# Expert weight buffers in two halves, one for each matmul, each refilled behind its own last use

## The chip, the cores and the metric

The kernel runs on one core of a Trainium2 chip. The metric is the device time of one execution in microseconds (us). A core has TensorE (PE in the profile; its weight loads are PEld), VectorE (DVE), ScalarE (ACT), GpSimd (POOL) and SyncE (SP), and 16 DMA engines that they share. SP and POOL issue the transfers here; each works through its own instructions in order, waits included.

## The reference

An attention with polynomial features feeds a mixture of experts, where each token goes to one expert.

```python
def _attn_ref(q, k, v, S1, S2):            # (4, 4, 1088, 32); S1, S2 (8, 32)
    phi = lambda x: outer(x @ S1.T, x @ S2.T)          # 64 features
    num = phi(q) @ (phi(k).T @ v)
    den = phi(q) @ phi(k).sum(seq) + 1e-6
    return num / den

def _moe_ref(x, w_gate, w_output_gate, w1, w2):   # x (4352, 128), E = 8, F = 1024
    logits = x @ w_gate
    e_idx = argmax(logits, axis=1)
    gate_w = softmax(logits)[e_idx]
    eom = sigmoid(x @ w_output_gate)
    for e in range(E):
        mask = e_idx == e
        h = maximum(x[mask] @ w1[e], 0)          # 128 -> 1024
        out[mask] = gate_w[mask] * eom[mask, e] * (h @ w2[e])   # 1024 -> 128
    return out
```

## The kernel before

The first part (to about 130 us) loads q, k and v in groups of columns, forms the attention output, computes the gates, and scatters each token's row, with its coefficient and its number, into a scratch array `xs` in HBM that is sorted by expert. A table is then made that says for each of `NT` = 41 tiles of 128 rows which expert it belongs to (`eti`) and where its rows begin (`bti`).

The second part walks over these 41 tiles with an order written out by hand. For each tile t:

- `rows(t)` (line 492, SP): reads the row address from `bti` (line 486) and loads 128 rows of 520 bytes into one of seven `xin` buffers. A buffer is free again when the scatter of the tile that used it has landed.
- `weights(t)` (line 496, SP): reads the expert from `eti` (line 486) and loads both weight matrices of the expert, 1 MB in 128 rows of 8 KB, into `wt[t % 3]`. The transfer has a condition: it is skipped when the buffer holds that expert already, that is when tile t-3 had the same one.
- `turn(t)` (line 502): TensorE transposes the rows, VectorE copies them to SBUF (line 504).
- `up(t)` (line 511): eight chunks of the first product into PSUM, read from `wt[t % 3][:, 0]`; then the relu on ScalarE (even tiles, line 513) or VectorE (odd tiles, line 515).
- `down(t)` (line 521): eight accumulating chunks of the second product, from `wt[t % 3][:, 1]`; ScalarE scales the result (line 523), and POOL scatters it to the output (line 524).

Each chunk of a product appears as two matmul instructions in the trace, so an up or a down has 16. The order for TensorE and SP is

```python
turn(0); turn(1); up(0)
for t in range(NT):
    turn(t + 2); up(t + 1); down(t)
    rows(t + NX)        # NX = 5
    weights(t + NW)     # NW = 3
```

Ahead of it stand `rows` 0 to 4 and `weights` 0 to 2 on SP, in turns. The three buffers are filled with the first expert's weights long before, at line 145, behind the loads of q, k and v.

Of the kernel before, what the change touches and what calls it, by code (L numbers as in the profile page):

```python
# [11 lines left out]
F32 = mybir.dt.float32  # L12
# [8 lines left out]
NW = 3  # L21
# [9 lines left out]
def kernel(  # L31
# [12 lines left out]
    nc = tc.nc  # L44
# [4 lines left out]
    E = w_d.shape[0]  # L49
    FC = (w_d.shape[2] // 2) // 128  # L50
# [9 lines left out]
    NT = (N + E * (TS - 1)) // TS  # L60
    PR = E * TS // 128

    consts = ctx.enter_context(tc.tile_pool(name="consts", bufs=1))
# [6 lines left out]
    def ps_t(name):  # L70
        return psum.tile([128, 512], F32, tag="t", bufs=2, name=name)

    def ps_w(name):
        return psum.tile([128, 2, 512], F32, tag="w2", bufs=2, name=name)

    def apart(group, ins):

        tc.declare_no_dep(ins.ins, group=group, reason="the rows are distinct")
        tc.add_to_no_dep_group(group, ins.ins)
# [8 lines left out]
    for i, x in enumerate((S1, S2)):  # L88
        own = slice(i * r, (i + 1) * r)
        if wide:  # L90
            x, dst, n = x.bitcast(I32), bits[own].rearrange("p (h d) w -> p h (d w)", h=2), 2 * D
# [48 lines left out]
            load_k(lead + g)  # L140


    wt = [consts.tile([128, 2, FC, 128], F32, tag=f"wt{i}", name=f"wt{i}") for i in range(NW)]
    for i in range(NW):
        nc.sync.dma_start(wt[i].rearrange("p a c x -> p (a c x)"), w_d[0])


    ident = consts.tile([128, 128], F32, tag="ident")
# [67 lines left out]
    ps = ps_t("ps_rows")  # L216
# [251 lines left out]
    eti = consts.tile([128, NT], I32, tag="eti")  # L468
# [14 lines left out]
    regs, xin, xTs, hTs = {}, {}, {}, {}  # L483

    def value(tab, t, top):
        return nc.values_load(tab[0:1, t:t + 1], engines=[mybir.EngineType.SP], min_val=0, max_val=top,
                              skip_runtime_bounds_check_because="the table is made within the bounds")

    def rows(t):
        at = value(bti, t, E * CAP - TS)  # L490
        xin[t] = work.tile([TS, W], F32, tag="xin", bufs=NX + 2, name="xin")
        nc.sync.dma_start(xin[t], xs[bass.ds(at, TS), :])

    def weights(t):
        regs[t] = value(eti, t, E - 1)
        nc.sync.dma_start(wt[t % NW].rearrange("p a c x -> p (a c x)"),
                          w_d[bass.ds(regs[t], 1)].rearrange("e p x -> p (e x)"),
                          cond=regs[t] != (regs[t - NW] if t >= NW else 0))

    def turn(t):  # L500
        ps = ps_t("ps_xs")[:, :TS]
        nc.tensor.transpose(ps, xin[t][:, :DM], ident)  # L502
        xTs[t] = work.tile([128, TS], F32, tag="xsT", bufs=3, name="xsT")
        nc.vector.tensor_copy(xTs[t], ps)  # L504

    def up(t):
        xT = xTs.pop(t)
        hTs[t] = work.tile([128, FC, TS], F32, tag="hT", name="hT")
        ps = ps_w("ps_h").rearrange("p a (c x) -> p (a c) x", x=TS)
        for c in range(FC):  # L510
            nc.tensor.matmul(ps[:, c], wt[t % NW][:, 0, c], xT, start=True, stop=True)  # L511
        if t % 2 == 0:
            nc.scalar.activation(hTs[t], ps, ACTF.Relu)  # L513
        else:
            nc.vector.tensor_scalar_max(hTs[t], ps, 0.0)  # L515

    def down(t):
        hT, x = hTs.pop(t), xin.pop(t)
        ps = psum.tile([TS, DM], F32, tag=("kvz", "rt")[t % 2], name="ps_y")
        for c in range(FC):  # L520
            nc.tensor.matmul(ps, hT[:, c], wt[t % NW][:, 1, c], start=(c == 0), stop=(c == FC - 1))  # L521
        y = work.tile([TS, DM], F32, tag="y", bufs=4, name="y")
        nc.scalar.activation(y, ps, ACTF.Copy, scale=x[:, DM:DM + 1])  # L523
        apart("out", nc.gpsimd.indirect_dma_start(  # L524
            out=out, out_offset=bass.IndirectOffsetOnAxis(ap=x.bitcast(I32)[:, DM + 1:DM + 2], axis=0),
            in_=y, in_offset=None, bounds_check=N - 1, oob_is_err=False))
# [3 lines left out]
    with tc.manual_schedule():  # L530
        for t in range(NX):
            rows(t)
            if t < NW:
                weights(t)
        turn(0)
        turn(1)
        up(0)
        for t in range(NT):
            if t + 2 < NT:
                turn(t + 2)  # L540
            if t + 1 < NT:
                up(t + 1)
            down(t)
            if t + NX < NT:
                rows(t + NX)
            if t + NW < NT:
                weights(t + NW)


# [34 lines left out]
```

## Time and profile before

| | |
|---|---|
| runs | 337.04, 331.01, 336.64 us; median 336.64 |
| profiled execution | 331.39 us, span 329.7 us, mean granted clock of TensorE 0.943 |
| TensorE busy | 270.0 us, 82% of the span |
| expert loop | about 139 to 322 us of the span |
| transfers | 44.49 MB in 18604 packets |

The span runs from the first to the last instruction of the core; the profiled execution's time has a little more around it. The granted clock is TensorE's, as a share of its full 2.4 GHz: 1.00 is 2.4 GHz and 0.50 is 1.2 GHz. In the chain of waits the pieces on TensorE lie end to end; in the timeline neighbouring matmuls overlap by a little, so that the same 16 matmuls show 1.79 us there and 1.95 us here. The name that a view gives for the releaser is inferred: at line 496 it names the transpose (line 502) that starts as the last matmul of a down ends.

### The profile page before, as it was taken

What the parts mean: (1) busy time and instruction counts of PE and PEld (TensorE: products, weight loads), DVE (VectorE), ACT (ScalarE), POOL (GpSimd) and SP (SyncE); (2) the same over time, 40 slices, a digit from 0 to 9 for tenths busy, and PEclk for the clock granted to TensorE, in tenths of its full rate; (3) what the DMA queues carried; (4) which work ended last, traced back from release to release, by engine and by line L of the source; (5) the groups of instructions that cost most, each with busy time, mean ns of one, the idle gap of its engine ahead of it and who ended that gap; (6) DMA issues with size and microseconds to landing.
All of it is one profiled execution on the core that took longest, in us unless ns stands there. A gap on an engine that the chain in (4) does not pass through costs nothing.

```text
span 329.7 us, 5562 instructions
## 1 busy us (share of the span) xinstructions
PE 270.0 (82%) x1990; PEld 245.2 (74%) x1990; DVE 103.3 (31%) x402; ACT 57.5 (17%) x108; POOL 77.9 (24%) x108
## 2 busy tenths in 40 slices
PE   1997899999999951199879888968978988889990
PEld 1996477778876651199869787858878988789990
DVE  4201235666566668022212112212111312222210
ACT  1000112212222110013112222202112222222220
POOL 3000001342334447112212221121122222212321
PEclk9999999999999965589979999989999999999995
DMA  5999998100010101212833748484473175671000
GB/s 149 252 252 245 245 245 354 35 32 10 25 35 24 35 33 48 90 40 81 262 126 101 243 134 278 151 288 140 136 227 110 45 230 204 187 253 34 16 2 0
DMA packets 18604, 44.49 MB, mean 135 GB/s; under 512 B 3258, under 2 KB 9148, under 8 KB 15504
## 3 DMA queue, kind: packets, MB, share of 16 engines
q1 hardware_dynamic: 16032, 39.09, 40.5%
q0 software_dynamic: 2544, 5.03, 4.4%
q8 instruction: 16, 0.26, 0.4%
q14 instruction: 12, 0.10, 0.1%
HBM read 60.06 MB, written 5.48 MB: 199 GB/s over the span
## 4 chain that ended last, share of the span: by engine, by line
PE 57%; DMA 25%; issue 7%; DVE 4%; POOL 3%; SPq 1%; ACT 1%; POOLq 0%; ACTq 0%
DMA wt<-in_w_dram 21%; PE ps_h L511 14%; PE ps_y L521 11%; PE ps_kvz L276 7%; PE ps_ab L249 6%; PE ps_nd L314 5%; PE ps_fa L294 5%; PE ps_fb L294 5%; PE ps_l L334 2%; POOL out_dram L524 2%; DMA xin<-xs 2%; DMA kT<-in_k_dram 1%; DMA xs<-pad,pai 1%; DVE kp L255 1%; PE ps_xt L329 1%
## 5 line engine op out<-in xcount | busy, mean ns | idle before, releaser
L511 PE MATMUL ps_h<-xsT,wt 128*128 128x128 f32 x656 | 85.2, 286 | 21.7 <-DMA wt<-in_w_dram 21.6
L511 PEld LDWEIGHTS ps_h<-xsT,wt 128*128 128x128 f32 x656 | 80.4, 200 | 25.4 <-issue 14.5
L521 PE MATMUL ps_y<-wt,hT 128*128 128x128 f32 x656 | 80.2, 276 | 0.0
L521 PEld LDWEIGHTS ps_y<-wt,hT 128*128 128x128 f32 x656 | 77.0, 193 | 0.0
L524 POOL DMA_INDIRECT out_dram<-y,xin x41 | 39.8, 971 | 149.9 <-ACT y L523 127.4
L396 POOL DMA_INDIRECT xs<-x,sloti x34 | 33.8, 995 | 93.9 <-DVE sloti L386 60.9
L504 DVE COPY xsT<-ps_xs 128x128 f32<-128x128 f32 x41 | 12.0, 292 | 105.2 <-PE ps_xs L502 105.2
L515 DVE TENSOR_SCALAR hT<-ps_h 128x1024 f32<-128x1024 f32 x20 | 24.5, 1225 | 41.8 <-PE ps_h L511 41.8
L513 ACT ACTIVATE hT<-ps_h 128x1024 f32<-128x1024 f32 x21 | 21.5, 1024 | 66.7 <-PE ps_h L511 66.7
L523 ACT ACTIVATE y<-ps_y,xin 128x128 f32<-128x128 f32 x41 | 15.1, 368 | 93.1 <-PE ps_y L521 93.1
L276 PEld LDWEIGHTS ps_kvz<-vt,kp 128*128 128x128 f32 (+1 forms) x144 | 22.8, 241 | 7.5 <-DVE kp L255 4.1
L276 PE MATMUL ps_kvz<-vt,kp 128*128 128x65 f32 (+1 forms) x144 | 23.7, 327 | 3.8 <-DVE kp L255 3.2
L502 PE MATMUL ps_xs<-ident,xin 128*128 128x128 f32 x41 | 11.6, 282 | 13.7 <-DMA xin<-xs 13.7
L249 PEld LDWEIGHTS ps_ab<-S12blk,kT 128*128 128x128 f32 x136 | 20.8, 241 | 2.5 <-DVE stepT L188 2.0
L249 PE MATMUL ps_ab<-S12blk,kT 128*128 128x32 f32 x136 | 20.9, 316 | 1.9 <-DMA kT<-in_k_dram 1.9
L294 PE MATMUL ps_fa<-qT,Sa 128*128 128x512 f32 (+1 forms) x36 | 19.1, 644 | 0.0
L314 PE MATMUL ps_nd<-kz,qp 128*128 128x66 f32 (+1 forms) x144 | 18.0, 273 | 0.1
L314 PEld LDWEIGHTS ps_nd<-kz,qp 128*128 128x128 f32 (+1 forms) x144 | 16.5, 186 | 1.6 <-issue 1.0
L294 PE MATMUL ps_fb<-qT,Sb 128*128 128x512 f32 (+1 forms) x36 | 17.3, 605 | 0.0
L255 DVE TENSOR_TENSOR kp<-ps_ab,b_sb 128x1024 f32<-128x1024 f32 (+1 forms) x9 | 10.5, 1166 | 21.7 <-ACT b_sb L252 21.7
L502 PEld LDWEIGHTS ps_xs<-ident,xin 128*128 128x128 f32 x41 | 6.0, 145 | 14.1 <-DMA xin<-xs 14.1
L306 DVE TENSOR_TENSOR qp<-a_sb,ps_fb 128x1024 f32<-128x1024 f32 (+1 forms) x9 | 10.5, 1161 | 12.8 <-PE ps_fb L294 12.8
(117 smaller groups left out, 146.8 us busy)
## 6 DMA issues: line engine op xcount, KB each, us to landing
wt<-in_w_dram SPq DMA_DIRECT2D x44, 1024.0 KB
kT<-in_k_dram SPq DMA_DIRECT2D x16, 256.0 KB, 8.8
qT<-in_q_dram SPq DMA_DIRECT2D x16, 256.0 KB, 7.5
xin<-xs SPq DMA_DIRECT2D x41, 65.0 KB, 4.0
vt<-in_v_dram SPq DMA_DIRECT2D x8, 260.0 KB, 6.2
out_dram<-y,xin POOLq DMA_INDIRECT x41, 4.5
xs<-x,sloti POOLq DMA_INDIRECT x34, 2.3
kT<-in_k_dram SPq DMA_DIRECT2D x2, 128.0 KB
```

The lines of the kernel that those rows point to most:

```text
L249: nc.tensor.matmul(ps[:, j * H + 2 * p:j * H + 2 * p + 2], kT[:, p, c * 128:(c + 1) * 128], S12blk, start=True, stop=True)
L276: nc.tensor.matmul(acc[b][:, p], s["kp"][p0:p0 + np_, j * H + 2 * p:j * H + 2 * p + 2].rearrange("s h i j -> s (h i j)"), vt[p0:p0 + np_, ...
L294: nc.tensor.matmul(ps[:, p, :n], S_.rearrange("p h i j -> p (h i j)"), qT[:, p, cols(cs)], start=True, stop=True)
L314: nc.tensor.matmul(ps[p0:p0 + np_, p, j], s["qp"][:, p, j * 128 + p0:j * 128 + p0 + np_], kvz_done[b][:, p], start=True, stop=True)
L396: apart("rows", nc.gpsimd.indirect_dma_start(out=xs[:, :], out_offset=bass.IndirectOffsetOnAxis(ap=sloti[:, j:j + 1], axis=0), in_=s["x"][ ...
L502: nc.tensor.transpose(ps, xin[t][:, :DM], ident)
L511: nc.tensor.matmul(ps[:, c], wt[t % NW][:, 0, c], xT, start=True, stop=True)
L513: nc.scalar.activation(hTs[t], ps, ACTF.Relu)
L515: nc.vector.tensor_scalar_max(hTs[t], ps, 0.0)
L521: nc.tensor.matmul(ps, hT[:, c], wt[t % NW][:, 1, c], start=(c == 0), stop=(c == FC - 1))
L523: nc.scalar.activation(y, ps, ACTF.Copy, scale=x[:, DM:DM + 1])
L524: apart("out", nc.gpsimd.indirect_dma_start(out=out, out_offset=bass.IndirectOffsetOnAxis(ap=x.bitcast(I32)[:, DM + 1:DM + 2], axis=0), in ...
```

## The change

Each buffer becomes two tiles, `wt[i][0]` for the first product and `wt[i][1]` for the second, 4 KB a partition each. `weights(t, a)` loads one half: 512 KB in 128 rows of 4 KB out of rows of 8 KB. The first half of tile t+4 is issued behind `up(t+1)`, the second half of tile t+3 behind `down(t)` and `rows(t+5)`. The expert is read from the table once, with the first half; both halves have the condition. The three preloads become six.

```diff
-    wt = [consts.tile([128, 2, FC, 128], F32, tag=f"wt{i}", name=f"wt{i}") for i in range(NW)]
+    wt = [[consts.tile([128, FC, 128], F32, tag=f"wt{a}{i}", name=f"wt{a}{i}") for a in range(2)] for i in range(NW)]
+
+    def half(a):
+        return slice(a * FC * 128, (a + 1) * FC * 128)
     for i in range(NW):
-        nc.sync.dma_start(wt[i].rearrange("p a c x -> p (a c x)"), w_d[0])
+        for a in range(2):
+            nc.sync.dma_start(wt[i][a].rearrange("p c x -> p (c x)"), w_d[0, :, half(a)])
...
-    def weights(t):
-        regs[t] = value(eti, t, E - 1)
-        nc.sync.dma_start(wt[t % NW].rearrange("p a c x -> p (a c x)"),
-                          w_d[bass.ds(regs[t], 1)].rearrange("e p x -> p (e x)"),
+    def weights(t, a):
+        if a == 0:
+            regs[t] = value(eti, t, E - 1)
+        nc.sync.dma_start(wt[t % NW][a].rearrange("p c x -> p (c x)"),
+                          w_d[bass.ds(regs[t], 1), :, half(a)].rearrange("e p x -> p (e x)"),
                           cond=regs[t] != (regs[t - NW] if t >= NW else 0))
...
-            nc.tensor.matmul(ps[:, c], wt[t % NW][:, 0, c], xT, start=True, stop=True)
+            nc.tensor.matmul(ps[:, c], wt[t % NW][0][:, c], xT, start=True, stop=True)
...
-            nc.tensor.matmul(ps, hT[:, c], wt[t % NW][:, 1, c], start=(c == 0), stop=(c == FC - 1))
+            nc.tensor.matmul(ps, hT[:, c], wt[t % NW][1][:, c], start=(c == 0), stop=(c == FC - 1))
...
             rows(t)
             if t < NW:
-                weights(t)
+                weights(t, 0)
+                weights(t, 1)
         turn(0)
         turn(1)
         up(0)
+        weights(NW, 0)
         for t in range(NT):
             if t + 2 < NT:
                 turn(t + 2)
             if t + 1 < NT:
                 up(t + 1)
+                if t + 1 + NW < NT:
+                    weights(t + 1 + NW, 0)
             down(t)
             if t + NX < NT:
                 rows(t + NX)
             if t + NW < NT:
-                weights(t + NW)
+                weights(t + NW, 1)
```

## Rows read from the trace of the kernel before

**Rows 1.** The page, parts 1 and 2: busy time and tenths in 40 slices.
```profile
PE 270.0 (82%) x1990; PEld 245.2 (74%) x1990; DVE 103.3 (31%) x402; ACT 57.5 (17%) x108; POOL 77.9 (24%) x108
PE   1997899999999951199879888968978988889990
```
**Rows 2.** The page, part 4: the chain of waits by line.
```profile
DMA wt<-in_w_dram 21%; PE ps_h L511 14%; PE ps_y L521 11%; PE ps_kvz L276 7%; PE ps_ab L249 6%; PE ps_nd L314 5%; PE ps_fa L294 5%; PE ps_fb L294 5%; PE ps_l L334 2%; POOL out_dram L524 2%; DMA xin<-xs 2%; DMA kT<-in_k_dram 1%; DMA xs<-pad,pai 1%; DVE kp L255 1%; PE ps_xt L329 1%
```
**Rows 3.** Waits on TensorE, 139 to 322 us: us in total, times, longest.
```profile
PE ps_h L511 <- DMA wt<-in_w_dram: 21.6, 16, 3.1
```
**Rows 4.** The SP queue's own waits, whole span.
```profile
SPq L496 <- PE ps_xs L502: 87.7, 38, 4.4
SPq L486 <- DVE bti L480: 83.6, 1, 83.6
SPq L492 <- DMA out_dram<-y,xin: 17.5, 17, 2.4
```
**Rows 5.** The chain in order of time, from 139 us: start, us, what.
```profile
139.83 2.94 PE ps_h L511 x16
...
150.14 0.11 PE ps_xs L502
150.25 1.79 PE ps_h L511 x16
152.03 1.79 PE ps_y L521 x16
...
153.85 4.82 DMA wt<-in_w_dram
158.67 0.14 issue
158.80 2.02 PE ps_h L511 x16
```
**Rows 6.** The two longest waits: chain, timeline, and a stretch (clock 0.50, DMA, GB/s).
```profile
168.87 3.24 PE ps_h L511 x16
172.11 2.20 PE ps_y L521 x16
...
213.86 6.71 DMA wt<-in_w_dram
...
220.71 3.62 PE L511 MATMUL ps_h<-xsT,wt 128*128 128x128 f32 x16 [3.09 <-DMA wt<-in_w_dram]
...
221.00:222.00 1.00, 1.00 (x6) 1.00 (x6) 0.00 (x0) 0.00 (x0) 0.00 (x0) 0.50 0.88 346
```
**Rows 7.** Weight issues in the SP timeline: skipped first, then first and last real.
```profile
136.80 0.11 SPq L496 DMA_DIRECT2D wt<-in_w_dram  x1
...
153.85 0.33 SPq L496 DMA_DIRECT2D wt<-in_w_dram  x1
...
291.86 0.33 SPq L496 DMA_DIRECT2D wt<-in_w_dram  x1
```
**Rows 8.** DMA: packets, then issues by line (count, KB each, us to landing).
```profile
DMA packets 18604, 44.49 MB, mean 135 GB/s; under 512 B 3258, under 2 KB 9148, under 8 KB 15504
...
kT<-in_k_dram SPq DMA_DIRECT2D x16, 256.0 KB, 8.8
xin<-xs SPq DMA_DIRECT2D x41, 65.0 KB, 4.0
```
**Rows 9.** Stretches: length; busy PE, PEld, DVE, ACT, POOL; clock, DMA share, GB/s.
```profile
10.00:20.00 10.00, 10.00 (x48) 10.00 (x49) 2.45 (x2) 0.53 (x2) 0.00 (x0) 1.00 1.07 250
142.60:153.80 11.20, 11.20 (x103) 11.20 (x102) 3.33 (x5) 2.79 (x4) 1.96 (x2) 1.00 0.16 37
196.00:210.70 14.70, 12.45 (x108) 11.82 (x107) 3.62 (x6) 2.50 (x5) 3.75 (x4) 1.00 0.74 240
252.00:264.00 12.00, 12.00 (x110) 12.00 (x110) 3.15 (x5) 3.12 (x5) 2.91 (x3) 1.00 0.13 35
...
200.50:201.00 0.50, 0.00 (x0) 0.00 (x0) 0.00 (x0) 0.00 (x0) 0.50 (x1) 1.00 1.37 266
201.00:201.50 0.50, 0.30 (x3) 0.33 (x4) 0.00 (x0) 0.00 (x0) 0.47 (x1) 1.00 0.94 147
201.50:202.00 0.50, 0.50 (x7) 0.50 (x6) 0.00 (x0) 0.00 (x0) 0.00 (x0) 1.00 0.57 164
```
**Rows 10.** Timeline: the last output copy.
```profile
320.99 0.37 ACT L523 ACTIVATE y<-ps_y,xin 128x128 f32<-128x128 f32 x1 [1.42 <-PE ps_y L521]
```
**Rows 11.** Single lines: duration in ns min/median/max, first and last start.
```profile
L521 PEldq EVENT_SEMAPHORE  x19: 51/51/51, 153.6 to 315.2; - x19
...
L496 SPq ALU_OP  x82: 37/39/54, 136.4 to 308.8; - x82
...
L486 SPq TENSOR_LOAD <-eti x41: 262/269/388, 136.1 to 308.4; - x41
```
**Rows 12.** The chain and the timeline just ahead of the first up.
```profile
136.06 0.28 SPq L486
...
139.35 0.47 PE ps_xs L502
```

## Prediction

> **What bounds the kernel now.** I read the page's first two parts first [rows 1]: TensorE (PE) is busy for 82% of the span, and its tenths fall below 9 mostly in the middle (the hand-over between the two halves of the kernel) and then again and again in the second half. The chain of waits [rows 2] names the cause: 21% of it is the transfer of expert weights (`wt<-in_w_dram`). That transfer exists only in the expert loop, so everything is decided in the stretch from about 139 us to 322 us. There [rows 3] the first product of the experts (line 511) waited 16 times for weights, 21.6 us together, the longest 3.1 us. The SP queue's own view [rows 4] shows the other end: SP stood 87.7 us at the weight issue (line 496) until TensorE was done with the buffer, and 17.5 us at the row loads (line 492) until an earlier scatter of results had landed.
>
> The chain in order of time tells how one stall is made [rows 5]. Without loads a tile costs 1.79 us for the first product ("up"), 1.79 for the second ("down"), and 0.11 for the transpose of the next rows ("turn"), 3.69 in all. At 153.85, when a down ends, a load is issued; it lands 4.82 us later and 0.14 us after that the up starts. Between the end of down(t), where the buffer comes free, and the start of up(t+3), which needs it, stand only turn, up, down, turn: 2 x 1.79 + 2 x 0.11 = 3.80 us. A load of about 5 us doesn't fit there, so nearly each pays about 1.1 to 1.4 us, and one that took 6.71 us paid 3.09 [rows 5, 6]. A stall costs more than the wait: the up after it shows 2.02 us in the chain instead of 1.79, and after the two longest waits 3.24 and 3.62 us [rows 6], at a granted clock of 0.50 (1.2 GHz instead of 2.4), after TensorE had stood idle.
>
> How many loads there are: of 41 weight issues those with unchanged expert are skipped. The real ones take about 0.33 us on SP, the skipped ones 0.08 to 0.11; the first and last real ones are at 153.85 and 291.86, and there are 21, three for each of seven experts (the first expert's are all skipped) [rows 7]. The packets agree: 18604 - 15504 = 3100 packets have 8 KB or more, and 24 loads (3 preloads and 21) x 128 rows of 8 KB are 3072, with 28 instruction packets the rest [rows 8]. From the order of real and skipped issues the experts have 5, 5, 4, 4, 4, 7, 4 and 8 tiles (the last with padding).
>
> **The change, part by part.**
>
> *Removed: the weight stalls.* A half of the first product is free at the end of up(t) and needed at up(t+3): three downs, two ups and three turns lie between, 5 x 1.79 + 3 x 0.11 = 9.28 us. The half of the second product is free at the end of down(t) and needed at down(t+3): three ups, two downs, three turns, again 9.28 us. Against 3.80 before, the time in hand is 5.5 us larger for both, and what must arrive first is half as large.
>
> What a half takes: in 196.0 to 210.7 three loads ran; the 16 DMA engines were busy 0.74 x 14.7 = 10.9 us [rows 9]. Row loads and scatters alone cost 0.13 x 12 = 1.56 us in 252 to 264, with 3.26 tiles, so 0.48 us a tile [rows 9]; four tiles take 1.9. The three loads are left with 9.0 us, 3.0 each, 1.5 for a half. The latency around it is 4.82 - 3.0 = 1.8 us [rows 5]. Alone a half lands 3.3 us after its issue, behind one other half 4.8, with a slow case like that of 6.71 us (1.9 more) 6.7: all under 9.28. So I take the remaining weight stall as zero. The bound on the other side: a half is moved in rows of 4 KB instead of 8, and the nearest row with smaller ones is the input stage, 2 KB rows (256 KB in 128 rows) at 250 GB/s with the engines full [rows 8, 9]. At that rate a half takes 0.524 MB / 250 = 2.1 us. Four-tile experts then need 6 x 2.1 + 1.9 = 14.5 us of engine time in 4 x 3.69 = 14.7 us: just full, and queues grow. I price that at up to 1.5 us for each of the four experts with four tiles: 0 to 6 us. I take 0, as 4 KB lies between the two rows, and even 2.1 us behind another 2.1 and 1.8 of latency are 6.0 of the 9.28 us.
>
> *The sum, end to end.* The first up starts its chain piece at 139.83 and takes 2.94 us (cold) [rows 5]. After it TensorE owes 40 ups, 41 downs and 39 turns: 81 x 1.79 + 39 x 0.11 = 149.3 us, so it is done at 142.77 + 149.3 = 292.1. Before, the last output copy, which starts as TensorE ends, began at 320.99 [rows 10]. Gain: 28.9 us. The stalls added up give nearly the same: 21.6 waits [rows 3], 14 x 0.23 = 3.2 for the slow ups, 1.45 + 0.41 + 1.83 = 3.7 for the work at the low clock [rows 5, 6], together 28.5. That no other engine is late next is shown by the stretches without loads: in 142.6 to 153.8 and 252 to 264 TensorE is busy throughout at 3.69 us a tile with the same relu, copies and scatters around it [rows 9]. What TensorE is fed from stays below that: SP's work per tile is two loads of a table value (0.27 each), the row issue (0.33) and now two weight issues with two ALU steps, a fused one and a move each (0.33 + 0.17), about 2.0 of 3.69 us [rows 11].
>
> *Added: a second skipped issue ahead of the loop.* Rows(1) stand behind weights(0) on SP, and up(0) behind turn(1). From the end of the table load (136.34) to the end of the skipped issue (136.91) 0.57 us pass [rows 7, 12]; the second half repeats that without the load. Bounds 0 and 0.6; I take +0.5, on the path, as TensorE waited for those rows until 139.35 [rows 12].
>
> *Added: a wait on TensorE for the second half* ahead of each down. A separate wait instruction is 51 ns; 19 of the 41 downs carry one already [rows 11], and the steady stretches show the same 1.79 with and without. Bounds 0 and 41 x 0.051 = 2.1 us; I take 0, since those rows are the nearest.
>
> *Moved: row loads.* Rows(t+5) now stand behind the first half's issue, so half a tile later (about 1.8 us), and the second half's issue stands behind them and behind their wait for the scatter of tile t-2, at most 2.4 us [rows 4]. Rows are needed three tiles on, 9.3 us, against 4.0 us to land [rows 8]; a second half 2.4 us late still has 6.9 us for 4.8. Being later, that wait is also shorter. Cost 0; without that cover it would be at most those 2.4 us a tile. The three preloads become six, on SP ahead of an 83.6 us wait for the tile table [rows 4]; cost 0.
>
> Span: 329.7 - 28.9 + 0.5 = 301.3. The profiled execution took 331.39, 1.7 us around its span, which gives **303.0 us**. It lies at the low end of the runs shown (331.01 to 337.04, median 336.64); the profile doesn't show where the other 5 us arise, so the range keeps them.
>
> **A rule that speaks against it.** The trace shows that loads don't pay their latency one after the other: from 200.5 to 202.0, while one 1 MB load lands at 201.1 and the next follows, the DMA share is 1.37, 0.94 and 0.57 and never near 0, and input loads of 256 KB land 8.8 us after issue while the queue moves 250 GB/s, which is several in flight [rows 8, 9]. The Trainium skill, page "DMA: Bandwidth & Descriptors", section "Rules for kernel authors", asks for at least 1 MiB per DMA, and its section "Anatomy of one DMA — SWDGE (gpsimd) path" gives each a fixed 2.0 us besides its bytes. By that figure, if nothing overlapped, an estimate for a half is 3.2 us, and the sum would be close to rival 1's. The overlap in the trace says that this isn't paid here.
>
> **The rivals.**
> 1. *Halves go one at a time, each with its own latency.* A half then holds the queue for 1.8 + 1.5 = T = 3.3 us, six for an expert 19.8 us against 14.7 for four tiles. From the first release (end of up(2): 142.77 + 3 x 1.79 + 2 x 0.11 + 0.5 = 148.9) 42 halves follow, with a pause at the seven-tile expert (25.8 - 6T), then one down and five tiles (20.2): TensorE ends at 194.9 + 36T = 313.7 instead of 321.0, the time is 324, at the edge of 2%; I count it as no change. Against it: the overlap above.
> 2. *The same, with the 2 KB rows' rate: slower.* T = 1.8 + 2.1 = 3.9, end at 335.3, so 14 us later than now: 346 us. The mechanism decides from T = 3.5 us on, where 194.9 + 36T equals 321.0. For it: small rows do move slower here (250 GB/s against 1.05 MB in 3.0 us, 350). Against it: the same overlap.
> 3. *Pipelined, but the engines are full with 4 KB rows*: 303 + 6 = 309 us, to 313. For it: the share of 0.74 already at four-tile experts.
> 4. *The change doesn't do what it says*: the first half is issued only when the down ends, SP being held. Then its room is 3.80 us again; a half alone takes 3.3, the second isn't needed before 5.6. Only the two slow loads would stall, with their cold clock: 303 + 3 = 306 us. For it: SP's in-order waits. Against it: every wait ahead on SP ends earlier on TensorE.
>
> **How the numbers follow.** Forecast 303 (300 to 308): 0.79. Rival 4: 0.06. Rival 3: 0.08. Rival 1: 0.04. Rival 2: 0.03. The range runs from 299 (the floor of TensorE's work less a little at the start) to 313, taking in rivals 3 and 4, the 2.1 us of waits and the spread of the runs; 0.93 by the cases. Faster by over 2%: 0.93; within 2% (about what a measurement of this kernel can tell from no change), rival 1: 0.04; slower: 0.03.
>
> **What would show it.** Right: TensorE's waits for weights fall from 21.6 us to under 3, all ups and downs after the first take 1.79 us in the chain, the clock stays at 1.00 from 143 us on, packets of 8 KB are gone and 48 x 128 of 4 KB appear, issues of first halves start at the end of ups, the DMA share in four-tile experts stays near 0.75. Wrong: waits at line 521 for weights, a share near 1 there (rival 3), landings that follow one another by over 3 us (rivals 1, 2), first halves issued at the end of downs (rival 4), or row loads that TensorE waits for.

## The result and the profile after

The change is faster: 307.92 us median (306.46 to 311.55, 4 runs) against 333.82 (329.04 to 337.04, 4 runs) in the same session; before has 334.95 over the eleven runs that were made with the last experiments (329.80 to 337.53). The ratio is 0.933 (95% interval 0.925 to 0.940), made from the undisturbed runs of each kernel alone (329.04 and 331.01 us against 306.46 to 308.40, on average 22.6 us apart), while the profiles of "before, again" and of the two kernels with the halves together, below, come from slower runs. The forecast was 303.0 against a profiled 331.39, which is 28.4 us and a ratio of 0.914. So direction and kind are right and the time lies in the range, 5 us above the forecast, at the upper end of the likeliest part of it (300 to 308).

The page of the changed kernel, parts 1 and 2 (busy time, tenths, granted clock; beside [rows 1]), and its DMA line ([rows 8]):

```profile
PE 265.9 (87%) x1990; PEld 243.1 (80%) x1990; DVE 103.3 (34%) x402; ACT 57.5 (19%) x108; POOL 77.5 (25%) x108
...
PE   0997979999999988402999999999999999999980
...
PEclk9999979899999999655899999999999999999997
DMA packets 22062, 44.50 MB, mean 146 GB/s; under 512 B 3642, under 2 KB 9532, under 8 KB 22032
```

From the twentieth slice on TensorE shows nothing but nines, up to the tail: the expert loop has no holes left. All packets are now under 8 KB. 22062 - 18604 = 3458 packets are new: 24 x 128 = 3072 from cutting each load in two, 3642 - 3258 = 384 of under 512 B (24 x 16, that is 16 for each of the 24 more transfers), and two of instructions. But the clock line has two dips in the first part, in the sixth and the eighth slice, that before's page hadn't.

The groups of instructions on TensorE by line (busy us, mean ns | idle before), and the SP queue's own waits from 144 to 290 us, beside [rows 3] and [rows 4]:

```profile
L516 PE MATMUL ps_h<-xsT,wt 128*128 128x128 f32 x656 | 81.8, 279 | 0.0
L526 PE MATMUL ps_y<-wt,hT 128*128 128x128 f32 x656 | 79.8, 275 | 0.0
```

```profile
SPq L501 <- PE ps_h L516: 15.8, 17, 1.1
SPq L501 <- PE ps_xs L507: 14.9, 36, 3.3
SPq L589 <- DMA out_dram<-y,xin: 11.5, 1, 11.5
SPq L496 <- ACT hT L518: 3.8, 14, 0.4
```

TensorE's wait for weights is 0.0 where it was 21.6 us. SP now waits for the end of ups (`ps_h`) as well as of downs, which is the first half being issued behind its own last use. And the 17.5 us that SP stood at the row loads for a scatter are gone: what is left there is 3.8 us on the relu's engine. That row becomes important below.

Two stretches of the expert loop (columns as in [rows 9]), the first over one four-tile expert:

```profile
182.70:197.40 14.70, 14.70 (x134) 14.70 (x133) 3.62 (x6) 3.52 (x6) 3.85 (x5) 1.00 0.81 244
148.00:298.00 150.00, 149.00 (x1334) 148.81 (x1333) 35.86 (x59) 36.34 (x62) 39.14 (x41) 1.00 0.59 180
```

In 14.7 us TensorE is busy for 14.7 us, at clock 1.00: the loop is bound by TensorE alone. The DMA share at a four-tile expert is 0.81; with 1.9 us for rows and scatters a half costs (0.81 x 14.7 - 1.9) / 6 = 1.67 us of engine time.

Where the 5 us went shows in the timeline at the seam (beside [rows 10] and [rows 12]):

```profile
139.63 0.36 SPq L496 DMA_DIRECT2D xin<-xs  x1
...
144.14 3.62 PE L516 MATMUL ps_h<-xsT,wt 128*128 128x128 f32 x16
...
297.04 0.37 ACT L528 ACTIVATE y<-ps_y,xin 128x128 f32<-128x128 f32 x1 [1.42 <-PE ps_y L526]
```

I cut each execution there, at the issue of the first sorted rows. Before, the first part took 135.66 us and the loop, up to the last output copy, 320.99 - 135.66 = 185.3. After, it is 139.63 and 297.04 - 139.63 = 157.4. The loop gained 27.9 us (forecast 28.9 - 0.5 = 28.4); the first part, in which no engine but SP has other instructions, lost 4.0; together that is 23.9. So two questions are left: what makes the gain in the loop, and whether the change or chance made the first part longer.

### The profile page after: what moved, and what is told of

It reads as the page before. It is cut to its first block, busy times and chain, and to the rows that moved or that the text cites. A ratio compares the mean times of both kernels' runs of the same rounds, so it can differ in the third digit from the quotient of the medians.

```text
span 305.7 us, 5829 instructions
## 1 busy us (share of the span) xinstructions
PE 265.9 (87%) x1990; PEld 243.1 (80%) x1990; DVE 103.3 (34%) x402; ACT 57.5 (19%) x108; POOL 77.5 (25%) x108
## 2 busy tenths in 40 slices
DMA packets 22062, 44.50 MB, mean 146 GB/s; under 512 B 3642, under 2 KB 9532, under 8 KB 22032
## 4 chain that ended last, share of the span: by engine, by line
issue 39%; PE 35%; POOL 13%; DVE 4%; DMA 3%; POOLq 1%; ACT 1%; SPq 1%; ACTq 0%
POOL out_dram L529 12%; PE ps_kvz L280 7%; PE ps_ab L253 6%; PE ps_fa L298 6%; PE ps_nd L318 6%; PE ps_fb L298 4%; PE ps_l L338 3%; DMA kT<-in_k_dram 1%; DMA xs<-pad,pai 1%; PE ps_xt L333 1%; POOLq L529 1%; PE ps_pos L372 1%; DVE kp L259 1%; DMA xin<-xs 1%; PE ps_pos L373 1%
## 5 line engine op out<-in xcount | busy, mean ns | idle before, releaser
L516 PE MATMUL ps_h<-xsT,wt 128*128 128x128 f32 x656 | 81.8, 279 | 0.0
L516 PEld LDWEIGHTS ps_h<-xsT,wt 128*128 128x128 f32 x656 | 78.4, 196 | 0.0
L280 PEld LDWEIGHTS ps_kvz<-vt,kp 128*128 128x128 f32 (+1 forms) x144 | 23.5, 245 | 8.1 <-DVE kp L259 4.4
L253 PEld LDWEIGHTS ps_ab<-S12blk,kT 128*128 128x128 f32 x136 | 20.8, 241 | 2.6 <-DVE stepT L192 2.1
L298 PE MATMUL ps_fa<-qT,Sa 128*128 128x512 f32 (+1 forms) x36 | 21.9, 728 | 0.0
L507 PEld LDWEIGHTS ps_xs<-ident,xin 128*128 128x128 f32 x41 | 6.0, 148 | 14.7 <-DMA xin<-xs 14.7
```

The costliest lines, as they stand in the source:

```text
L253: nc.tensor.matmul(ps[:, j * H + 2 * p:j * H + 2 * p + 2], kT[:, p, c * 128:(c + 1) * 128], S12blk, start=True, stop=True)
L280: nc.tensor.matmul(acc[b][:, p], s["kp"][p0:p0 + np_, j * H + 2 * p:j * H + 2 * p + 2].rearrange("s h i j -> s (h i j)"), vt[p0:p0 + np_, ...
L298: nc.tensor.matmul(ps[:, p, :n], S_.rearrange("p h i j -> p (h i j)"), qT[:, p, cols(cs)], start=True, stop=True)
L516: nc.tensor.matmul(ps[:, c], wt[t % NW][0][:, c], xT, start=True, stop=True)
```

## Experiments

Each kernel's loop is cut in the same way. "Waits" is TensorE's wait for weights in the loop.

| kernel | first rows issued | last output copy | loop | waits | time, median |
|---|---|---|---|---|---|
| before | 135.66 | 320.99 | 185.3 | 21.6 | 334.95 |
| before, again | 144.89 | 326.09 | 181.2 | 18.3 | 336.56 (one) |
| after | 139.63 | 297.04 | 157.4 | 0 | 307.92 |
| after, again | 143.50 | 300.40 | 156.9 | 0 | 310.80 (one) |
| split, halves together | 141.59 | 307.59 | 166.0 | 5.5 | 314.23 |
| the same, ten row buffers | 144.64 | 305.75 | 161.1 | 1.9 | 314.94 |
| split, second half first | 142.98 | 337.91 | 194.9 | 27.6 | 349.30 |
| four whole buffers | 141.30 | 298.61 | 157.3 | 0 | 309.05 |
| change, 2 KB rows | 139.41 | 295.92 | 156.5 | 0 | 307.52 |
| change, early start | 139.26 | 295.02 | 155.8 | 0 | 306.91 |

**Both kernels once more, for the first part.** No edit. Expected of before:

> The kernel before once more, for its first part alone. In the profiles so far the load of the first sorted rows is issued at 135.66 us before the change and at 139.63 us after it, though no instruction of TensorE stands in another order there. Theory 'by chance': the first part differs from execution to execution, because the granted clock falls at other places; this repeat lies anywhere from 134 to 142 us. Theory 'by the change' (six preloads of 512 KB in place of three of 1 MB): it lies at 135.7 within 1 us, and its first part has no stretch at clock 0.50 between 10 and 115 us. The expert loop, from that issue to the last output copy, is 185 us within 3 by both.

And of after:

> The kernel after the change once more, for its first part alone. Theory 'by chance': the issue of the first sorted rows lies anywhere from 134 to 142 us. Theory 'by the change': at 139.6 within 1 us, with stretches at a low clock around 42 and 53 us again. The expert loop from there to the last output copy is 157.4 us within 1 by both.

Measured: the first rows are issued at 144.89 us in before and at 143.50 in after. Both lie above the 134 to 142 us that "by chance" had expected, and before's loop of 181.2 us lies outside 185 within 3; after's 156.9 is as expected. The theory "by the change" fails all the same: the kernel with three whole preloads took 9.2 us longer than its first profile, more than the one with six halves, and the one with four whole preloads (below) came to 141.30. Two stretches of before's first profile, and then the same two of its repeat (columns as in [rows 9]; the last three are clock, DMA share, GB/s):

```profile
42.00:44.00 2.00, 2.00 (x11) 1.28 (x10) 0.00 (x0) 0.00 (x0) 0.00 (x0) 1.00 1.12 252
10.00:116.00 106.00, 101.08 (x597) 81.00 (x597) 51.14 (x226) 18.54 (x40) 23.49 (x24) 1.00 0.52 135
```

```profile
42.00:44.00 2.00, 2.00 (x4) 0.97 (x4) 0.00 (x0) 0.00 (x0) 0.00 (x0) 0.50 1.09 223
10.00:116.00 106.00, 100.15 (x548) 78.78 (x549) 46.06 (x202) 16.43 (x35) 19.60 (x20) 0.94 0.52 133
```

Same kernel, same work: at 42 us the clock is 1.00 in one and 0.50 in the other (1.2 instead of 2.4 GHz), and over 10 to 116 us the mean is 1.00 against 0.94. At half clock for 12% of 106 us that is 12.7 us at half speed, some 6.4 us of work, if TensorE sets the pace there. That would account for most of the 9.2 us; TensorE's last matmul of that part starts at 124.6 us in one and 132.3 in the other.

Over all ten profiled executions the first rows are issued from 135.66 to 144.89 us: with whole preloads at 135.66, 141.30 and 144.89, with halves at 139.26 to 144.64. By and large, the later they are, the lower is the mean clock over 10 to 116 us: 1.00 at 135.66, 0.97 at 139.26 to 139.63, 0.95 at 141.30 and 141.59, and 0.92 to 0.94 from 142.98 on. The first fall also comes ahead of what the change alters. Here are the stretch and the first preload, of the change and then of the kernel with four whole buffers:

```profile
42.40:45.70 3.30, 3.30 (x5) 1.24 (x5) 0.00 (x0) 0.00 (x0) 0.00 (x0) 0.50 1.11 241
...
46.08 5.14 SPq L149 DMA_DIRECT2D wt<-in_w_dram  x6
```

```profile
40.40:46.60 6.20, 6.20 (x19) 4.13 (x18) 0.00 (x0) 0.79 (x1) 0.00 (x0) 0.50 1.10 231
...
46.68 3.35 SPq L145 DMA_DIRECT2D wt<-in_w_dram  x4
```

Nine of the ten profiles are at 0.50 from 42.9 to 43.7 us, and no preload is issued before 45.4, so preloads, whole or halved, don't make this fall. The tenth, with no such stretch up to 110 us and the shortest first part of all, is the profile on which the forecast rests. That the clock accounts for the longer first part is read from these ten executions; no run changed the clock alone.

**Halves together, where the whole load stood.** Does the gain need the first half's own place, or does splitting the buffer do it?

```diff
                 up(t + 1)
-                if t + 1 + NW < NT:
-                    weights(t + 1 + NW, 0)
             down(t)
             ...
             if t + NW < NT:
+                weights(t + NW, 0)
                 weights(t + NW, 1)
```

(`weights(NW, 0)` ahead of the loop goes too.)

> Split buffers, but both halves are issued one behind the other where the whole load stood, behind down(t) and rows(t+5). Theory 'room': the first half needs no place of its own, as its buffer is free since up(t) and SP comes to it about 1.2 us after down(t-1); its room is 9.3 - 1.8 - 1.2 = 6.3 us against 3.3 to 4.9 to land, so TensorE waits for weights under 1 us in all and the expert loop takes 157 to 159 us, the whole some 307 us. Rival 'place': without its own place behind the up the first half comes with the second at the end of the down, room 3.8 us; the slower loads stall, 5 to 15 us in all, the loop takes 163 to 175 us.

Measured: the loop takes 166.0 us and TensorE waits 5.5 us for weights; ratio 0.940 (0.926 to 0.955). The theory "room" as I priced it fails, and "place" fits the numbers. The reason stands in the SP queue's waits of this kernel from 140 to 300 us:

```profile
SPq L501 <- PE ps_xs L507: 38.9, 32, 3.0
SPq L496 <- DMA out_dram<-y,xin: 20.8, 16, 2.4
```

and in its timeline at one of the six stalls, first SP, then TensorE:

```profile
182.54 2.06 SPq L501 DMA_DIRECT2D wt<-in_w_dram  x2
185.68 0.33 SPq L496 DMA_DIRECT2D xin<-xs  x1
186.69 1.59 SPq L501 DMA_DIRECT2D wt<-in_w_dram  x2
...
192.43 2.02 PE L516 MATMUL ps_h<-xsT,wt 128*128 128x128 f32 x16 [0.72 <-DMA wt<-in_w_dram]
```

The pair at 182.54 is done at 184.60. The row load behind it goes only at 185.68, when the scatter that holds its buffer has landed, and the next first half at 186.69. It lands 5.6 us later (0.14 us ahead of the up's start at 192.43), and TensorE has stood 0.72 us. So SP was held by the scatter with the weights queued behind, and the landing, 5.6 us, is longer than the 3.3 to 4.9 that I had.

**The same with ten row buffers**, so that the row load doesn't wait for the scatter:

```diff
-        xin[t] = work.tile([TS, W], F32, tag="xin", bufs=NX + 2, name="xin")
+        xin[t] = work.tile([TS, W], F32, tag="xin", bufs=NX + 5, name="xin")
```

> Both halves behind down(t) and rows(t+5) as in the run before, but ten row buffers in place of seven. There the SP queue stood 20.8 us in 16 waits at the row loads until a scatter had landed, with both weight halves queued behind, and TensorE waited 5.5 us for weights. Theory 'held': that wait is what made the first halves late; with ten buffers it is gone, SP issues the first half some 1.2 us after down(t-1), TensorE waits under 1 us and the loop takes 157 to 158.5 us instead of 166.0. Rival 'place': the first half is late since it has no place behind the up; TensorE still waits 4 to 7 us and the loop stays at 163 to 168.

Measured: the wait for scatters is gone from SP's view, TensorE's waits for weights fall from 5.5 to 1.9 us, the loop to 161.1. TensorE's wait in that kernel:

```profile
PE ps_h L516 <- DMA wt<-in_w_dram: 1.9, 6, 1.0
```

Neither expectation is met in full: without the hold 3.6 of the 5.5 us are gone, and the other 1.9 stays with the later place, where the room is 9.28 - 1.79 - 1.3 = 6.2 us, about a landing under load. By their times alone (ratios 0.940 and 0.941, with intervals that overlap the change's) these two kernels can't be told from each other or from the change. There is one profile of each, in which the clock is 1.00 from 155 to 300 us, so I use the waits for what they name and not for exact sizes.

**Second half first.** The first half can't be issued before the down ends:

```diff
             if t + NW < NT:
                 weights(t + NW, 1)
+                weights(t + NW, 0)
```

(with the first half's place behind the up removed, and the table read by whichever comes first)

> Split buffers with the second half issued ahead of the first on SP, both where the whole load stood: the first half then can't be issued before down(t) ends, though it is as small as in the change. Theory 'room': it is issued 0.6 us after the end of down(t) and lies behind the other half on the DMA engines, so it lands about 0.6 + 1.8 + 1.6 + 1.6 = 5.6 us after it, against a room of 3.8: stalls of 1 to 2 us for each load come back, 20 to 35 us in all, the loop takes 178 to 195 us, the whole some 328 to 345 us. Rival 'size' (the gain comes from transfers of half the size, which land sooner): it lands 3.5 to 4 us after the down, stalls under 5 us in all, loop under 163 us, the whole under 314 us.

Measured: 349.30 us, ratio 1.054 (1.042 to 1.066), loop 194.9:

```profile
PE ps_h L516 <- DMA wt<-in_w_dram: 27.6, 18, 2.7
```

One of its stalls, first SP, then TensorE:

```profile
189.31 1.04 SPq L501 DMA_DIRECT2D wt<-in_w_dram  x2
...
194.85 2.02 PE L516 MATMUL ps_h<-xsT,wt 128*128 128x128 f32 x16 [1.78 <-DMA wt<-in_w_dram]
```

The pair is issued as a down ends, and the first half has landed 0.14 us ahead of 194.85, 5.4 us after the pair's start; a whole load took 4.82 [rows 5]. Transfers of half the size, the same buffers, the same bytes, and the kernel is slower than the one before, as the first half now lands later than the whole load did. That refutes "size" and, with the four whole buffers below, shows the main cause: what counts is when the first half lands against the up that needs it, and that follows from when and behind what SP issues it. The time lies a little above the expected 345, with 18 waits of 1.5 us.

**Four whole buffers.** The rival way to get room:

```diff
-NW = 3
+NW = 4
```

> The kernel before with four whole 1 MB buffers in place of three, nothing split: the room of a load grows by a tile, from 3.8 to 7.5 us, but an expert of four tiles or more now takes four loads, 28 in all. Theory 'room': loads land 4.8 to 6.5 us after issue, so stalls are under 3 us in all, the loop takes 157 to 161 us and the whole some 308 us, as with the change. Rival 'capacity': four-tile experts need 4 x 3.0 + 1.9 = 13.9 of 14.7 us on the DMA engines, queues grow, 5 to 15 us of stalls, loop 163 to 175 us, the whole 314 to 326.

Measured: no wait for weights, loop 157.3 us, ratio 0.931 (0.923 to 0.939): the same as the change. One four-tile stretch of it:

```profile
184.37:199.07 14.70, 14.70 (x135) 14.70 (x134) 3.62 (x6) 3.51 (x6) 3.89 (x4) 1.00 0.89 317
```

The engines are busy to 0.89 with 28 MB of loads instead of 21, and TensorE still never waits. "Capacity" fails. SP waited 42.3 us for scatters here and it cost nothing, as a load has 7.5 us of room and stands where SP must wait for the down anyway. This kernel also speaks on the size of transfers: 1 MB or 512 KB, the loop is 157.3 or 157.4. In engine time the halves do cost more: a whole load takes (0.89 x 14.7 - 1.9) / 4 = 2.8 us, two halves 2 x 1.67 = 3.3. The Trainium skill, page "DMA: Bandwidth & Descriptors", section "Rules for kernel authors", asks for at least 1 MiB per DMA where bandwidth is the goal. These shares agree with it in direction; the loop doesn't show it, since TensorE bounds it at either share.

**2 KB rows.** The change, with the weights laid out in HBM as [expert, 4, 128, 512]:

```diff
-                          w_d[bass.ds(regs[t], 1), :, half(a)].rearrange("e p x -> p (e x)"),
+                          w_d[bass.ds(regs[t], 1), half(a)].rearrange("e k p x -> p (e k) x"),
```

> The change with the weights laid out in HBM so that a half is moved in rows of 2 KB in place of 4, by as many transfers of the same size. Theory 'row size' (the input loads with 2 KB rows moved 250 GB/s): a half takes 2.1 us of the DMA engines instead of the 1.67 that the change shows, four-tile experts come to 6 x 2.1 + 1.9 = 14.5 of 14.7 us, a share of 0.95 to 1 there; landings stay under the 9.28 us of room mostly, so stalls are 0 to 6 us, the loop takes 157 to 163. Rival 'size of the transfer decides, not the row': the share stays at 0.81 and the loop at 157.

Measured: the weights' packets did double (28206 in all), and TensorE waits for weights no more than in the change:

```profile
DMA packets 28206, 44.50 MB, mean 146 GB/s; under 512 B 3642, under 2 KB 9532, under 8 KB 28176
...
182.48:197.18 14.70, 14.70 (x135) 14.70 (x134) 3.61 (x6) 3.48 (x7) 3.88 (x4) 1.00 0.77 241
```

The share is 0.77, a little under the 0.81 of the change, and the loop takes 156.5 us. "Row size" fails: 2 KB rows alone are not what holds the input loads at 250 GB/s.

**Early start.** A version that might beat the change: its loop is bound by TensorE, but the first up waits for the second tile's rows.

```diff
             rows(t)
+            if 0 < t <= NW:
+                weights(t - 1, 1)
             if t < NW:
                 weights(t, 0)
-                weights(t, 1)
         turn(0)
-        turn(1)
         up(0)
+        turn(1)
```

> The change with another order ahead of the loop: up(0) right behind turn(0) on TensorE, and on SP rows(1) behind the first half of tile 0 alone, the other skipped issues after it. Before, up(0) starts 4.5 us after the issue of the first rows, as it stands behind turn(1) and so behind rows(1). Theory: up(0) then starts as soon as the first rows are turned, 2.7 us after that issue; the loop takes 155.4 us instead of 157.2, the whole about 1.8 us less than the change, some 306 us. Rival: the second rows or the skipped halves come late now and up(1) waits for them; no gain, loop 157 to 159.

Measured: 306.91 us, ratio 0.929 (0.923 to 0.936), against the change's 0.933.

```profile
139.26 0.36 SPq L496 DMA_DIRECT2D xin<-xs  x1
...
142.04 3.31 PE L516 MATMUL ps_h<-xsT,wt 128*128 128x128 f32 x16 [0.38 <-DVE xsT L509]
```

The first up starts 2.8 us after the first rows' issue instead of 4.5, and the loop takes 155.8 us, 1.1 to 1.6 less than in the change's two profiles. It is the shortest loop here; as a time the gain is inside the spread of the first part.

## Why the prediction came out as it did

- **Stalls removed, loop end to end.** Right. Forecast 185.3 - 28.4 = 156.9 us for the loop, measured 157.4 and 156.9. The waits for weights went from 21.6 to 0, and the ups at the low clock behind them are gone: the clock is 1.00 from 148 us on. The half microsecond over the forecast in the first profile arises at the start of the loop, where the clock is still at 0.50 until 148 us (143 was forecast) and the first up takes 3.62 us.
- **The sum, at "Span: 329.7 - 28.9 + 0.5".** Here lies the miss of 5 us. The mechanism held, but the gain was taken in full from one profile that was uneven in two ways. It had the shortest first part of all ten, 135.66 us, where the changed kernel's profiles have 139.63 and 143.50. It also had the longer of before's two profiled loops: 185.3 us with waits of 21.6, against 181.2 with 18.3. I had noted that this execution lay at the low end of the runs, but kept it as the likeliest. As a whole it was not unusual: 331.39 us, beside 329.04 and 331.01 for the runs that the ratio is made from. So the miss is not one of the base alone: those runs gained 22.6 us and not 28.4. Between the first profiles the loop gained 27.9 us and the first part lost 4.0; against the loop of before's repeat the gain is 24 us. With two profiles of before it stays open how much of the missing 5 us lies in the first part and how much in the loop. That 307.92 still falls inside 300 to 308 is in part luck: the upper end allowed for a spread of before's runs whose place I didn't know.
- **What a half takes.** 1.5 us of the engines forecast, 1.67 measured. Landing was mis-sized: 3.3 to 4.8, with a slow case of 6.7, while the late halves of the joint version show 5.6. The room of 9.28 us was wide enough that it didn't matter here; at 6.2 us of room it shows as stalls.
- **The upper bound by the 2 KB rows** (0 to 6 us). Taken as 0, rightly, but the bound was wrong in kind: rows of 2 KB cost nothing in this loop.
- **Second skipped issue, +0.5.** The first up starts 4.51 us after the first rows' issue instead of 3.96: 0.55.
- **Wait on TensorE ahead of each down, 0.** Right: TensorE is busy for 14.70 of 14.70 us, and the kernel with four whole buffers, which has no such second wait, has the same loop.
- **Row loads moved, 0.** Right in size, and worth more than I saw: standing half a tile later they no longer meet an unlanded scatter, and that keeps SP free for the halves. Without the first half's own place in front the same wait held SP for 20.8 us.
- **Rivals 1 and 2** (halves one at a time) and **3** (engines full): no sign. At four-tile experts six halves go through in 14.7 us, which is 2.45 us each and not 3.3, and even at a share of 0.89 nothing waits. The fixed 2.0 us behind the estimate for a half are stated in the Trainium skill, page "DMA: Bandwidth & Descriptors", section "Anatomy of one DMA — SWDGE (gpsimd) path", for transfers that GpSimd issues. The weights are issued by SP, so the figure needn't hold for them; no run here measures it.
- **Rival 4** didn't occur, but its price was wrong. I gave a first half that SP is held from issuing 3.3 us to land and only 3 us of loss in all. In the nearest run, halves together, SP is held for less than that rival assumes, landing took 5.6 us at the stall shown, and the loop is 8.6 us longer than the change's. Issued behind the other half, which was not among the rivals, it cost 27.6 us of waits and made the kernel slower than before.

Not settled: why the clock falls in the first part in some executions and not in others, with the same instructions on TensorE. No experiment here changes what TensorE does in that part.

## What to carry to other kernels

Reckon a prefetch by its room: the time from the buffer's last use to the next need, against the landing time under load, with what the issuing queue must wait for in between. Splitting a buffer by its users, or adding a buffer, both enlarge it, and here they come out the same; the order of issues on SP's queue decides whether the room is used. And before subtracting a gain from a profiled time, ask whether that execution's other parts are typical: one repeat of the unchanged kernel would have shown 9 us of difference in a part that the change hardly touches, and 4 us in the loop itself.

## What the hardware showed that I hadn't expected

- The first part of the same kernel differs by 9.2 us between two executions, with the mean granted clock over 10 to 116 us at 1.00 and 0.94.
- The input loads, in rows of 2 KB, move 250 GB/s with the engines full, while weight halves in rows of 2 KB take no more engine time than in rows of 4 KB (share 0.77 and 0.81 at a four-tile expert). The input loads of q and k write 64 partitions each and the weights 128; whether that is the cause wasn't tried.
